# Unread matmuls before the expert work, a new order and half tiles in the last expert, and three more DMA transposes

## The chip, the cores and the metric

The kernel runs on one core of one Trainium2 chip. The core has a matmul engine (TensorE; PE in the profile, with its weight loads as PEld), three engines for elementwise work (VectorE, DVE; ScalarE, ACT; GpSimd, POOL), a sync engine (SP) that mostly issues transfers, and 16 DMA engines. A stretch of queue of an engine is named by a q behind it (SPq). The metric is the time of one execution on the device in microseconds (us), the median of several runs.

## The reference

The first half is an attention with global and local tokens: 8 batches, 8 heads of 64, 32 global and 512 local tokens. A global query sees all keys; a local one sees the global keys and the local keys within 32 places. The second half is a mixture of 8 experts over all 4352 tokens, weighted by a Sinkhorn-normalised router:

```python
k_all = np.concatenate([k_g, k_l], axis=2)
out_g = np.matmul(sm(scale * q_g @ k_all^T), v_all)
mask = np.abs(pos[:, None] - pos[None, :]) <= 32
s_l = np.concatenate([scale * q_l @ k_g^T, np.where(mask, scale * q_l @ k_l^T, -1e9)], axis=-1)
out_l = np.matmul(sm(s_l), v_all)
...
P = np.exp(logits - logits.max())
for _ in range(8):
    P /= P.sum(1, keepdims=True) + 1e-09
    P /= P.sum(0, keepdims=True) + 1e-09
    P *= N / E
for e in range(E):
    out += P[:, e:e + 1] * (np.maximum(x @ w1[e], 0.0) @ w2[e])
```

(The matrix products are shortened here.) Each expert goes from 512 to 1024 to 512 features.

## The kernel before

**Layout.** The tokens stand in 34 tiles of 128: tiles 0 to 31 are the local tokens, four to a batch, and tiles 32 and 33 are the global tokens of all batches. `groups` (L75) makes nine groups of them: eight of four tiles, and group 8 of the two global tiles. `xT` holds the attention's result, turned; `out_nat` holds the sums of the experts in float32, 34 tiles of 128 by 512.

**The attention loop** (L446 to L565) works on 32 pairs of heads, in 35 turns with an order of its own that is written out by hand (`manual_schedule`): each engine runs its instructions in the order in which the loop issues them. In turn i the pair i is loaded and turned (`stage_aq`, `stage_ak`: L288 on TensorE, L293 on VectorE, L305 on ScalarE, and L309 on GpSimd for the zero-padded queries), pair i - 1 gets its scores (`stage_b`, L325 and L326 on TensorE, L329 on VectorE) and exponentials (`stage_e`, L339 on ScalarE), pair i - 2 has its exponentials turned, and pair i - 3 is multiplied with the values (`stage_c`, L365 on TensorE, L369 and L372 on VectorE) and turned back (`stage_d`, L380 and L381). Every second turn does the global queries: scores in even turns (`global_scores`, L387 and L395; `global_exp`, L402; `global_norm`, L409), the rest in odd ones (`global_turn`, L415; `global_out`, L430). In turn 1 VectorE also clears some buffers (L534 to L539).

**Turning the exponentials.** A pair has two heads, hi = 0 and 1. For pairs below `NPE` = 6 both heads are turned by TensorE (`stage_t`, L350, seven transposes), and copied out of PSUM by ScalarE (first head) or VectorE (second head), both in L352. From pair 6 on, `stage_e` issues a DMA transpose from SP (L343) as soon as the head's last exponential stands.

**The expert work in the attention loop.** `fill(1)` stands at eight places of each turn. It takes a piece (two matmuls of 512 columns) of the expert work in `queue`, if there is any. Expert 0's work on a batch enters the queue at the end of the turn that finishes the batch (L518), first in turn 6; so up to there the eight `fill(1)` do nothing. Its PSUM tiles come from the pool `ps_m`, two buffers under the tag `mo`.

**The experts.** Behind the loop come the router's normalisation, with expert work between its steps, and then experts 1 to 7 (L621 to L629). For each expert and each group, `layer1` (L94) makes eight tiles of hidden features, whose ReLU is done by ScalarE (L101) and VectorE (L103) in turns, and `layer2` (L114) makes, for each tile of tokens, eight matmuls of 512 columns into `py`. VectorE adds `py` times the router's weight to `out_nat` (L124). In the last expert `store_tile` then stores the tile from SP: a local tile by one transfer of 256 KB (L81), whose rows are ordered "(p s) d -> s p d" with s = 4 outermost, a global one by four of 64 KB (L85). An expert's weights (L71, L72) are loaded while the one before it computes.

The order of the experts' groups is 0 to 8 for every expert, so the two global tiles are last.

Of the kernel before, what the change touches and what calls it, by code (L numbers as in the profile page):

```python
# [11 lines left out]
FP32 = mybir.dt.float32  # L12
AF = mybir.ActivationFunctionType
ALU = mybir.AluOpType
# [3 lines left out]
P = 128  # L18
# [4 lines left out]
def kernel(  # L23
# [13 lines left out]
    nc = tc.nc  # L37

    B, H, Sl, Dh = q_l.shape
    Sg = q_g.shape[2]  # L40
    D, E = moe_w_gate.shape
# [4 lines left out]
    NJ = Sl // P  # L46
    DP = D // P
    TO = NTOK // P
    FT = F // P
# [11 lines left out]
    out_nat = persist.tile([P, TO, D], FP32)  # L61
    P_nat = persist.tile([P, TO, E], FP32)
    w_gate_sb = persist.tile([P, DP, E], FP16)
    identity = persist.tile([P, P], FP16)
# [9 lines left out]

    groups = [(4 * b, 4) for b in range(B)] + [(4 * B, TO - 4 * B)]  # L75

    def store_tile(t):
        if t < 4 * B:
            b, j = divmod(t, NJ)
            r0 = S * b + Sg + P * j  # L80
            nc.sync.dma_start(out=out[r0 : r0 + P, :].rearrange("(p s) d -> s p d", s=NJ), in_=out_nat[:, t, :])  # L81
        else:
            for i in range(4):
                b = 4 * (t - 4 * B) + i
                nc.sync.dma_start(out=out[S * b : S * b + Sg, :],  # L85
                                  in_=out_nat[Sg * i : Sg * (i + 1), t, :])
# [21 lines left out]
    def layer2(e, w2e, g, ps, tag, hT, copy):  # L108
        t0, gn = groups[g]
        for c in range(gn):  # L110
            t = t0 + c
            py = ps.tile([P, D], FP32, tag=tag, name=f"py{e}_{t}")
            for fk in range(FT):
                nc.tensor.matmul(py, hT[fk][:, P * c : P * (c + 1)], w2e[:, fk, :],  # L114
                                 start=(fk == 0), stop=(fk == FT - 1))
                if fk % 2 == 1 and fk < FT - 1:
                    yield
            if e == 0:
                if copy == "act":
                    nc.scalar.copy(out=out_nat[:, t, :], in_=py)  # L120
                else:
                    nc.vector.tensor_copy(out=out_nat[:, t, :], in_=py)  # L122
            else:
                nc.vector.scalar_tensor_tensor(out=out_nat[:, t, :], in0=py, scalar=P_nat[:, t, e : e + 1],  # L124
                                               in1=out_nat[:, t, :], op0=ALU.mult, op1=ALU.add)
                if e == E - 1:
                    store_tile(t)
            yield
# [3 lines left out]
        yield from layer1(e, wts[e][0], g, ps1, tag1, hp, hT, relu)  # L132
        yield from layer2(e, wts[e][1], g, ps2, tag2, hT, copy)

    queue = []

    def fill(n):
        while n > 0 and queue:
            if next(queue[0], "done") == "done":
                queue.pop(0)  # L140
            else:
                n -= 1

    make_identity(nc, identity)
    wts = [None] * E

    with ExitStack() as actx:
# [7 lines left out]
        ps_m = pool(name="ps_m", bufs=2, space=PSUM)  # L155
        actx.enter_context(tc.manual_schedule())

        NU, NK, NQ, VW, NPE = 4, 3, 2, Dh + 2, 6
        U7 = 7 * P
        OFF, WID = (0, 224, 480, 704), (192, 224, 224, 192)  # L160
        AV = ((("a", 0, 0), ("o", 0, 1)), (("o", 3, 1), ("a", 1, 2), ("o", 1, 3)),
# [99 lines left out]
        for (d0, n, c0, w) in ((0, NJ, WIN, P), (224, NJ - 1, 0, WIN), (128, NJ - 1, WIN + P, WIN)):  # L261
            nc.vector.tensor_copy(out=mgap[:, 0:n, d0 : d0 + w],
                                  in_=mcan[:, c0 : c0 + w].unsqueeze(1).broadcast_to([P, n, w]))
# [70 lines left out]
        def stage_e(p, hi, jp):  # L334
            st, nm = sts.pop((p, hi, jp))
            u = u_buf[(2 * p + hi) % NU]
            for jj in range(2):
                j = 2 * jp + jj
                nc.scalar.activation(out=u[:, OFF[j] : OFF[j] + WID[j]], in_=st[:, jj, 0 : WID[j]], func=AF.Exp,  # L339
                                     scale=-1.0, bias=nm[:, jj : jj + 1])  # L340
            if jp == 1 and p >= NPE:
                uT = awk.tile([P, 7, P], FP16, tag="uT", bufs=5, name=f"uT{p}_{hi}")
                nc.sync.dma_start_transpose(out=uT, in_=u)  # L343
                uTs[2 * p + hi] = uT
# [101 lines left out]
        for i in range(NP + 3):  # L446
# [2 lines left out]
            kt = (i - 3) // 2 if i >= 3 and i % 2 == 1 and (i - 3) // 2 < 2 * B else None  # L449
            ks = (i - 2) // 2 if i >= 2 and i % 2 == 0 and (i - 2) // 2 < 2 * B else None  # L450
            bv, x = divmod(i + 2, 4)
            V = 0 < bv < B

            if Bs:
# [2 lines left out]
            if Bs:  # L457
                stage_b(pb, 0, 1)
                stage_e(pb, 0, 0)
            if 0 <= i - 2 < NPE:  # L460
                stage_t(i - 2, 0)
            fill(1)
            if C:
                stage_c(pc)
            if Bs:
                stage_b(pb, 1, 0)
                stage_e(pb, 0, 1)
            if 0 <= i - 2 < NPE:
                stage_t(i - 2, 1)
            if i == 0:  # L470
                load_pair("k", k_l, 2)
# [3 lines left out]
            if A:  # L475
                stage_aq(pa)
                if i > 0:
                    order("q", i + 1)
            if V and x in (1, 2):
                load_va(bv, x + 1)  # L480
# [14 lines left out]
            if ks is not None:  # L495
                if ks == 0:
                    qg_transposes(qs)
                gsu[ks] = global_scores(ks)
            if V and x < 2:
                load_va(bv, x)  # L500
            if V and x == 3:
                load_vo_edges(bv)
# [40 lines left out]
            if i in (1, 2):  # L543
                c = slice(512 * (i - 1), 512 * i)
                nc.gpsimd.dma_start(out=wts[0][0][:, :, c], in_=moe_w1[0][:, c].rearrange("(dko dki) f -> dki dko f", dki=P))
            elif i in (4, 5):
                c = 4 * (i - 4)
                nc.gpsimd.dma_start(out=wts[0][1][:, c : c + 4, :],
                                    in_=moe_w2[0][P * c : P * (c + 4)].rearrange("(fko fki) d -> fki fko d", fki=P))
            if 8 <= i < 14:  # L550
                d, src = ((skg, k_g), (svg, v_g), (sqg, q_g))[(i - 8) // 2]
# [17 lines left out]
    with tc.tile_pool(name="wpool2", bufs=1) as wpool2, \  # L569
         tc.tile_pool(name="hx", bufs=34) as hx, \  # L570
         tc.tile_pool(name="ps_h", bufs=3, space=PSUM) as ps_h, \
         tc.tile_pool(name="ps_y", bufs=4, space=PSUM) as ps_y, \
         tc.tile_pool(name="ps_k", bufs=1, space=PSUM) as ps_k, \
         tc.manual_schedule():

        wts[1] = load_weights(1, wpool2)
        for g in range(B - 1, len(groups)):
            queue.append(both(0, g, ps_h, "ph", ps_y, "py", hx, "act", "act"))
        NPRE = 3
        pre = [[] for _ in range(NPRE)]  # L580
        for g in range(NPRE):
            queue.append(layer1(1, wts[1][0], g, ps_h, "ph", hx, pre[g], "act"))

        gm = sink.tile([P, 1], FP32, tag="gm")
        nc.vector.reduce_max(out=gm, in_=P_nat, axis=AX.XY)
        gmb = sink.tile([P, P], FP32, tag="gmb", bufs=1)
        nc.vector.tensor_scalar(out=gmb, in0=ones_mat, scalar1=gm, scalar2=None, op0=ALU.mult)
        fill(4)
        pgm = ps_k.tile([P, P], FP32, tag="pk", name="pgm")
        nc.tensor.matmul(pgm, gmb, ident32, start=True, stop=True)  # L590
        gma = sink.tile([P, 1], FP32, tag="gma")
        nc.vector.reduce_max(out=gma, in_=pgm, axis=AX.X)
        gmn = sink.tile([P, 1], FP32, tag="gmn")
        nc.vector.tensor_scalar(out=gmn, in0=gma, scalar1=-1.0, scalar2=None, op0=ALU.mult)
        fill(2)
        nc.scalar.activation(out=P_nat, in_=P_nat, func=AF.Exp, bias=gmn)

        ratio = float(NTOK) / float(E)
        for it in range(8):
            rs = sink.tile([P, TO, 1], FP32, tag="rs")  # L600
            nc.vector.reduce_sum(out=rs, in_=P_nat, axis=AX.X)  # L601
            nc.vector.tensor_scalar(out=rs, in0=rs, scalar1=1e-9, scalar2=None, op0=ALU.add)
            nc.vector.reciprocal(out=rs, in_=rs)  # L603
            nc.vector.tensor_tensor(out=P_nat, in0=P_nat, in1=rs.broadcast_to([P, TO, E]), op=ALU.mult)  # L604
            cp = sink.tile([P, E], FP32, tag="cp")
            nc.vector.reduce_sum(out=cp, in_=P_nat.rearrange("p t e -> p e t"), axis=AX.X)  # L606
            fill(8)
            pcs = ps_k.tile([P, E], FP32, tag="pk", name=f"pcs{it}")
            nc.tensor.matmul(pcs, ones_mat, cp, start=True, stop=True)  # L609
            fill(1)  # L610
            cr = sink.tile([P, 1, E], FP32, tag="cr")
            nc.vector.tensor_scalar(out=cr[:, 0, :], in0=pcs, scalar1=1e-9, scalar2=1.0 / ratio,
                                    op0=ALU.add, op1=ALU.mult)
            nc.vector.reciprocal(out=cr, in_=cr)
            nc.vector.tensor_tensor(out=P_nat, in0=P_nat, in1=cr.broadcast_to([P, TO, E]), op=ALU.mult)  # L615
        for t in range(TO):
            eng = nc.vector if t < 2 else nc.gpsimd
            eng.tensor_scalar(out=out_nat[:, t, :], in0=out_nat[:, t, :], scalar1=P_nat[:, t, 0:1],  # L618
                              scalar2=None, op0=ALU.mult)
        fill(1 << 30)  # L620
        for e in range(1, E):  # L621
            if e > 1:
                wts[e] = load_weights(e, wpool2 if e % 2 else wpool)
            for g in range(len(groups)):
                if e == 1 and g < NPRE:
                    queue.append(layer2(1, wts[1][1], g, ps_y, "py", pre[g], "dve"))
                else:
                    queue.append(both(e, g, ps_h, "ph", ps_y, "py", hx, "both"))
                fill(1 << 30)  # L629
# [30 lines left out]
```

## Time and profile before

| | |
|---|---|
| median of 3 runs | 1091.76 us (1091.75 to 1091.79) |
| the profiled execution | 1095.55 us, of which its span is 1093.7 |
| mean granted TensorE clock in it | 0.993 |
| TensorE busy | 1054.3 us (96%), 6734 matmuls |
| VectorE, ScalarE, GpSimd busy | 559.7, 331.1 and 239.6 us (51%, 30%, 22%) |
| all matmuls of `layer1` (L94) and of `layer2` (L114) | 499.1 and 495.9 us |
| DMA traffic | 56.27 MB, mean 51 GB/s |

The span runs from the first to the last instruction of the profiled execution. In the profile's tables a window row has its bounds and length, then for each engine its busy time and the number of instructions, then the granted clock (PEclk, 1.00 is full), the mean share of the 16 DMA engines that was busy (where it exceeds 1, transfers overlap on an engine), and GB/s. A timeline row has its start, its time, engine, line, operation, output and input, a count, and in brackets the idle time before it with what ended that. A row of waits has who waited for whom, the sum, the count and the longest.

### The profile page before, as it was taken

The page shows a single profiled execution, that of the slowest core. Times are in us where ns is not written, and L with a number is a line of the kernel's source. Part 1 is how long each engine was busy: PE and PEld are TensorE (multiplying, and loading weights), DVE is VectorE, ACT ScalarE, POOL GpSimd, SP SyncE. Part 2 cuts the span into 40 slices and gives each one's busy share as a digit, 9 for nine tenths or more (in the row PEclk, how much of TensorE's full clock was granted, in tenths as well). Part 3 has the DMA queues.
Part 4 walks back from the last instruction along what each step waited for, and adds up shares of the span by engine and source line. Part 5 has one row for each costly group of instructions (what it writes and reads, how often), then busy time and mean ns, then how long its engine had stood idle before and what let it go on. Part 6 is the DMA issues. An engine that isn't in the chain of part 4 may idle for free.

```text
span 1093.7 us, 17193 instructions
## 1 busy us (share of the span) xinstructions
PE 1054.3 (96%) x6734; PEld 540.0 (49%) x6734; DVE 559.7 (51%) x1361; ACT 331.1 (30%) x683; POOL 239.6 (22%) x300
## 2 busy tenths in 40 slices
PE   4799999999999999999999999999999999999997
PEld 3666666655444544445444544454444444454443
DVE  6888888867244444444444444444444444444443
ACT  6767777754311111112111111111111111111111
POOL 8977788610990000000000000000000000000000
PEclk9899999999999999999999999999999999999999
DMA  9999999951003030004000400022000400002222
GB/s 159 136 137 159 139 140 141 126 88 25 1 11 68 12 66 1 1 1 78 0 1 1 78 1 1 1 35 44 1 1 1 77 1 1 1 10 77 76 77 90
DMA packets 126210, 56.27 MB, mean 51 GB/s; under 512 B 90800, under 2 KB 117680, under 8 KB 126128
## 3 DMA queue, kind: packets, MB, share of 16 engines
q0 software_dynamic: 64304, 28.98, 22.4%
q1 hardware_dynamic: 60736, 25.53, 11.9%
q8 instruction: 53, 0.87, 0.3%
q10 hardware_dynamic: 1088, 0.66, 0.3%
q14 instruction: 29, 0.24, 0.1%
HBM read 60.31 MB, written 8.91 MB: 63 GB/s over the span
## 4 chain that ended last, share of the span: by engine, by line
PE 78%; DVE 1%; issue 0%; ACT 0%; ACTq 0%; DVEq 0%
PE py L114 39%; PE ph L94 39%; DVE st L329 0%; PE po L365 0%; PE pcs L609 0%; DVE cp L606 0%; DVE out_nat L122 0%; PE pog L430 0%; DVE P_nat L604 0%; DVE P_nat L615 0%; DVE rs L601 0%; PE px L380 0%; DVE rs L603 0%; DVE out_nat L124 0%; DVE gm L395 0%
## 5 line engine op out<-in xcount | busy, mean ns | idle before, releaser
L94 PE MATMUL ph<-xT,w1e 128*128 128x512 f16 (+1 forms) x2304 | 499.1, 368 | 0.4 <-DVE P_nat L442 0.4
L114 PE MATMUL py<-w2e,ht 128*128 128x512 f16 x2176 | 495.9, 379 | 0.0
L101 ACT ACTIVATE ht<-ph 128x512 f16<-128x512 f32 (+1 forms) x336 | 192.7, 573 | 686.5 <-PE ph L94 686.0
L94 PEld LDWEIGHTS <-w1e 128*128 128x128 f16 x2304 | 219.5, 98 | 220.6 <-issue 0.4
L114 PEld LDWEIGHTS <-ht 128*128 128x128 f16 x2176 | 207.3, 98 | 231.9
L124 DVE SCALAR_TENSOR_TENSOR out_nat<-py,P_nat,out_nat 128x512 f32<-128x512 f32 x238 | 178.6, 750 | 248.2 <-PE py L114 247.2
L103 DVE TENSOR_SCALAR ht<-ph 128x512 f16<-128x512 f32 (+1 forms) x240 | 158.5, 660 | 226.4 <-PE ph L94 224.6
L71 POOL DMA_DIRECT2D w1e<-in_moe_w_dram x7 | 5.4, 770 | 510.0 <-PE ph L94 505.4
L339 ACT ACTIVATE u<-st,nm 128x192 f16<-128x192 f32 (+1 forms) x256 | 104.0, 461 | 37.3 <-DVE nm L329 26.0
L329 DVE CUSTOM_DVE_ANT_0 st<-s,mask 128x192 f32<-128x192 f32 (+1 forms) x256 | 82.3, 368 | 4.7 <-PE s L326 3.1
L618 POOL TENSOR_SCALAR out_nat<-out_nat,P_nat 128x512 f32<-128x512 f32 x32 | 49.6, 1575 | 36.5 <-DVE P_nat L615 36.5
L325 PE MATMUL s<-kT,qTz 128*128 128x160 f16 (+1 forms) x256 | 44.7, 245 | 6.7 <-DVE nm L329 2.9
L309 POOL COPY qTz<-qT 64x512 f16<-64x512 f16 x60 | 36.7, 612 | 38.1 <-ACT qT L305 36.0
L326 PE MATMUL s<-kgT,qTz 128*128 128x32 f16 x256 | 37.1, 183 | 0.0
L325 PEld LDWEIGHTS <-qTz 128*128 128x128 f16 x256 | 25.9, 101 | 14.9 <-DVE nm L329 3.2
L326 PEld LDWEIGHTS <-qTz 128*128 128x128 f16 x256 | 25.0, 98 | 10.3 <-issue 2.2
L365 PEld LDWEIGHTS <-uT 128*128 128x128 f16 x640 | 24.4, 99 | 9.4 <-issue 3.1
L409 POOL TENSOR_SCALAR ug<-ug,gr 128x544 f16<-128x544 f16 x16 | 26.5, 1658 | 10.2 <-DVE gr L408 9.7
L197 POOL DMA_DIRECT2D va<-in_v_l_dram x32 | 28.7, 901 | 0.0
L365 PE MATMUL po<-va,uT 128*128 128x65 f16 x256 | 25.5, 196 | 2.0 <-ACT ug L402 1.9
L372 DVE TENSOR_TENSOR xn<-po,rc 128x512 f16<-128x512 f32 x32 | 22.1, 691 | 1.1
L293 DVE COPY kT<-pk 128x512 f16<-128x512 f16 x32 | 22.0, 686 | 0.2 <-PE pk L288 0.2
(107 smaller groups left out, 472.8 us busy)
## 6 DMA issues: line engine op xcount, KB each, us to landing
out_dram<-out_nat SPq DMA_DIRECT2D x32, 256.0 KB
w1e<-in_moe_w_dram POOLq DMA_DIRECT2D x7, 1024.0 KB, 7.9
w2e<-in_moe_w_dram POOLq DMA_DIRECT2D x7, 1024.0 KB, 10.1
va<-in_v_l_dram POOLq DMA_DIRECT2D x32, 128.0 KB, 4.7
kr<-in_k_l_dram POOLq DMA_DIRECT2D x30, 128.0 KB, 4.4
qr<-in_q_l_dram POOLq DMA_DIRECT2D x30, 128.0 KB, 4.5
w1e<-in_moe_w_dram POOLq DMA_DIRECT2D x2, 512.0 KB, 7.1
w2e<-in_moe_w_dram POOLq DMA_DIRECT2D x2, 512.0 KB, 7.3
```

What stands on the lines that cost most here:

```text
L94: nc.tensor.matmul(ph[:, 0:N], w1e[:, dk, P * fm : P * (fm + 1)], xT[:, dk, P * t0 : P * t0 + N], start=(dk == 0), stop=(dk == DP - 1))
L101: nc.scalar.activation(out=ht[:, 0:N], in_=ph[:, 0:N], func=AF.Relu)
L103: nc.vector.tensor_scalar(out=ht[:, 0:N], in0=ph[:, 0:N], scalar1=0.0, scalar2=None, op0=ALU.max)
L114: nc.tensor.matmul(py, hT[fk][:, P * c : P * (c + 1)], w2e[:, fk, :], start=(fk == 0), stop=(fk == FT - 1))
L124: nc.vector.scalar_tensor_tensor(out=out_nat[:, t, :], in0=py, scalar=P_nat[:, t, e : e + 1], in1=out_nat[:, t, :], op0=ALU.mult, op1=ALU.add)
L309: nc.gpsimd.tensor_copy(out=qTz_buf[2 * (p % NQ) + hi][r], in_=qT[r])
L325: nc.tensor.matmul(ps[:, jj, w0 : w0 + k1 - k0], lhsT, kT[:, k0:k1], start=True, stop=True)
L326: nc.tensor.matmul(ps[:, jj, g0 : g0 + Sg], lhsT, kg, start=True, stop=True)
L329: nc.vector.tensor_tensor_reduce(out=st[:, jj, 0 : WID[j]], in0=ps[:, jj, 0 : WID[j]], in1=mask[:, OFF[j] : OFF[j] + WID[j]], scale=-scale ...
L339: nc.scalar.activation(out=u[:, OFF[j] : OFF[j] + WID[j]], in_=st[:, jj, 0 : WID[j]], func=AF.Exp, scale=-1.0, bias=nm[:, jj : jj + 1])
L365: nc.tensor.matmul(po[:, hi, W * j : W * (j + 1)], uT[:, blk, :], v[:, x, 2 * hp + hi, 0:W], start=(n == 0), stop=(n == len(AV[j]) - 1))
L618: eng.tensor_scalar(out=out_nat[:, t, :], in0=out_nat[:, t, :], scalar1=P_nat[:, t, 0:1], scalar2=None, op0=ALU.mult)
```

## The change

There are three edits.

1. *Unread matmuls.* From turn 1 to turn 6, a `fill(1)` that finds no expert work issues four 128-column matmuls of the identity with itself into a tile of the pool `ps_m`. Nothing reads the result. That is 8 units a turn and 48 in all, 192 matmuls. In turn 7 the list is emptied.
2. *The last expert.* In expert 7 group 8, with the global rows, comes first, and groups 0 to 7 follow. The last tile is then tile 31; it is computed in two halves of 256 columns, each with its own eight matmuls, its own addition on VectorE and its own store of 128 KB.
3. *DMA transposes.* `NPE` becomes (6, 3): first heads are turned by TensorE up to the sixth pair as before, second heads only up to the third. So the second heads of pairs 3, 4 and 5 (counted from 0) go by DMA transpose from SP.

```diff
-    def store_tile(t):
+    def store_tile(t, c0=0, c1=D):
...
-            nc.sync.dma_start(out=out[r0 : r0 + P, :].rearrange("(p s) d -> s p d", s=NJ), in_=out_nat[:, t, :])
+            nc.sync.dma_start(out=out[r0 : r0 + P, c0:c1].rearrange("(p s) d -> s p d", s=NJ),
+                              in_=out_nat[:, t, c0:c1])
...
+            if e == E - 1 and t == 4 * B - 1:
+                for c0 in range(0, D, D // 2):
+                    h = slice(c0, c0 + D // 2)
+                    for fk in range(FT):
+                        nc.tensor.matmul(py[:, h], hT[fk][:, P * c : P * (c + 1)], w2e[:, fk, h],
+                                         start=(fk == 0), stop=(fk == FT - 1))
+                    nc.vector.scalar_tensor_tensor(out=out_nat[:, t, h], in0=py[:, h], scalar=P_nat[:, t, e : e + 1],
+                                                   in1=out_nat[:, t, h], op0=ALU.mult, op1=ALU.add)
+                    store_tile(t, c0, c0 + D // 2)
+                yield
+                continue
...
-    queue = []
+    queue, warming = [], []
...
+        while n > 0 and warming:
+            pw = warming[0].tile([P, 512], FP32, tag="mo", name=f"pw{len(warming)}")
+            warming.append(pw)
+            for c in range(4):
+                nc.tensor.matmul(pw[:, P * c : P * (c + 1)], identity, identity, start=True, stop=True)
+            n -= 1
...
-        NU, NK, NQ, VW, NPE = 4, 3, 2, Dh + 2, 6
+        NU, NK, NQ, VW, NPE = 4, 3, 2, Dh + 2, (6, 3)
...
-            if jp == 1 and p >= NPE:
+            if jp == 1 and p >= NPE[hi]:
...
+            if i == 1:
+                warming.append(ps_m)
+            elif i == 7:
+                warming.clear()
...
-            if 0 <= i - 2 < NPE:
+            if 0 <= i - 2 < NPE[0]:
                 stage_t(i - 2, 0)
...
-            if 0 <= i - 2 < NPE:
+            if 0 <= i - 2 < NPE[1]:
                 stage_t(i - 2, 1)
...
-            for g in range(len(groups)):
+            order_g = list(range(len(groups)))
+            for g in order_g if e < E - 1 else order_g[-1:] + order_g[:-1]:
```

## The prediction

> **What bounds the kernel now.** I read the page's slices first, then the windows cut at the turns of the attention loop, then TensorE's timeline, and for the end the SP queue's timeline, its waits and windows over the output stores.
>
> ```profile
> PEclk9899999999999999999999999999999999999999
> ```
>
> TensorE is busy 96% of the span, so two places are open: the first 60 us, where the granted clock falls, and what follows the last matmul. Turn i of the loop begins with its first score matmul (L325); the windows are turns 1 to 9 in order.
>
> ```profile
> core 0: us, PE busy (x) PEld busy (x) DVE busy (x) ACT busy (x) POOL busy (x), PEclk, DMA share, GB/s
> 9.71:13.77 4.06, 2.58 (x25) 2.16 (x25) 3.64 (x18) 3.66 (x8) 4.06 (x6) 1.00 1.36 143
> 13.77:22.90 9.13, 5.38 (x47) 4.18 (x46) 6.55 (x24) 6.65 (x17) 9.07 (x15) 1.00 1.62 158
> 22.90:30.47 7.57, 5.62 (x90) 5.15 (x89) 6.25 (x25) 5.66 (x14) 7.36 (x11) 0.77 1.18 135
> 30.47:35.62 5.15, 3.92 (x74) 3.33 (x69) 4.88 (x23) 4.07 (x10) 5.09 (x8) 1.00 1.38 159
> 35.62:42.77 7.15, 4.60 (x88) 3.94 (x88) 6.35 (x26) 5.29 (x13) 7.00 (x10) 1.00 1.00 105
> 42.77:49.44 6.67, 4.50 (x89) 3.81 (x85) 5.94 (x25) 4.96 (x12) 6.15 (x11) 0.93 1.21 184
> 49.44:59.54 10.10, 9.97 (x109) 7.16 (x106) 5.96 (x26) 6.24 (x15) 6.65 (x9) 0.71 0.80 94
> 59.54:65.56 6.02, 6.02 (x70) 3.88 (x69) 5.33 (x23) 5.33 (x13) 4.94 (x8) 1.00 1.39 153
> 65.56:72.98 7.42, 6.64 (x91) 4.48 (x90) 5.65 (x26) 5.28 (x14) 7.25 (x11) 1.00 1.22 149
> ```
>
> Turns 3 to 6 are VectorE's and GpSimd's (DVE 6.25 of 7.57, POOL 7.36 of 7.57); TensorE stands idle for 13.1 us of turns 1 to 6. From turn 7 on expert matmuls fill it, and turn 7 takes 10.10 us where turn 9, with the same kinds of steps, takes 7.42: its clock is 0.71, because the stretch before it was thin:
>
> ```profile
> 45.07:48.49 3.42, 1.88 (x23) 1.35 (x22) 3.42 (x12) 3.07 (x8) 3.02 (x5) 1.00 1.27 198
> ...
> 8.34 0.59 PE L288 MATMUL pk<-identity,k 128*128 128x128 f16 x4
> ...
> 34.44 0.38 PE L288 MATMUL pk<-identity,k 128*128 128x128 f16 x4 [0.62 <-ACT qT L305]
> ```
>
> The two rows of four 128-column matmuls are the same work at the half and the full clock (before 20 us the page has no clock record and prints 1.00; the durations say half). The end:
>
> ```profile
> 1067.30:1069.90 2.60, 2.60 (x13) 1.18 (x12) 0.92 (x2) 1.04 (x2) 0.00 (x0) 1.00 0.26 87
> 1069.90:1072.50 2.60, 2.60 (x14) 1.18 (x13) 1.16 (x2) 0.77 (x2) 0.00 (x0) 1.00 0.26 101
> 1072.50:1075.10 2.60, 2.60 (x14) 1.19 (x13) 0.94 (x2) 0.42 (x1) 0.00 (x0) 1.00 0.25 98
> 1075.10:1076.90 1.80, 1.80 (x10) 0.86 (x9) 0.82 (x2) 0.00 (x0) 0.00 (x0) 1.00 0.08 31
> ...
> 1074.86 0.75 DVE L124 SCALAR_TENSOR_TENSOR out_nat<-py,P_nat,out_nat 128x512 f32<-128x512 f32 x1 [1.03 <-PE py L114]
> ...
> 1075.63 0.54 SPq L81 DMA_DIRECT2D out_dram<-out_nat  x1
> ...
> 1080.81 0.54 SPq L81 DMA_DIRECT2D out_dram<-out_nat  x1
> ...
> 1086.98 0.75 DVE L124 SCALAR_TENSOR_TENSOR out_nat<-py,P_nat,out_nat 128x512 f32<-128x512 f32 x1 [0.98 <-PE py L114]
> ...
> 1090.47 0.32 SPq L85 DMA_DIRECT2D out_dram<-out_nat  x1
> ...
> SPq L85 <- DMA out_dram<-out_nat: 1.3, 1, 1.3
> ```
>
> The windows stand in a layer-1 stretch without new stores, after a group's four 256 KB stores, the last issued at 1067.00. They drain at some 100 GB/s with a DMA share of 0.25: four of 16 engines, 2.6 us a tile, while TensorE makes a tile in 1.73 us (L124 at 1061.04, 1062.77, 1064.49, 1066.22). So the fourth store is behind the other three. The last three lines price that: the store of tile 31, issued at 1080.81, is what the last L85 store waits for (same semaphore), until 1090.47, 9.66 us after its issue. That backlog now lies under the last group's 7 us of matmuls.
>
> **The change part by part.** The sum goes against the profiled execution (span 1093.7, 1.85 us around it, 1095.55 in all); the median is 3.79 below it, and I carry differences over unchanged.
>
> *Order and halves in the last expert.* TensorE: 16 matmuls of 256 columns for 8 of 512; L94's 256-column rows are 0.109 us apart (3.49 us for 32), 16 make 1.74 against 1.73: nothing. The global group after its own predecessor in expert 6 needs its activations (0.38 ACT, 0.42 DVE) in turns every 0.87 us: covered, and its eight 64 KB stores move ahead of the 32 tile stores on SP, which sits idle there: nothing. Expert 7's weights are asked for about 117 us earlier: nothing; without that cover a load shows 7.9 and 10.1 us. The cost is behind the last matmul. Tile 28's L124 now begins three tiles before the last, at 1086.98 - 3 x 1.73 = 1081.79, its store 0.77 later (1074.86 to 1075.63) at 1082.56. A whole tile 31 would land as long after it as now: 1090.47 - 1075.63 = 14.84, so at 1097.40. The halves are issued near 1086.8 and 1087.4, while the four engines work on tiles 29 and 30, so the earlier start buys nothing. No half store is in this trace. Bounds: half the time of a whole one each (2.6 together, landing 1097.4) to as long as a whole one each (5.2, landing 1100.0). The DMA packet records have 84 ns for the stores' 2 KB packets and 46 to 54 ns for 1 KB packets of the first loads; 32 packets an engine at 46 to 54 give 1.5 to 1.7 a half, 2.9 to 3.5 the pair: landing 1097.7 to 1098.3; I take 1098.0. What SP, GpSimd and the barrier do behind the last landing takes 1.6 us now (landing record 1092.1, end 1093.7), 1.35 with the last store's semaphore last in SP's row of waits: end 1099.4. **Term: +5.7 us** (bounds +5.0 and +7.9).
>
> The Trainium skill (DMA: Bandwidth & Descriptors, "Why a DMA increments its semaphore by 16 and not by 1") says that a hardware-queue copy uses the largest number of engines up to 16 that divides both sides' slowest dimension, and the lowest-numbered ones: four for [4, 32, 256] as for [4, 32, 512]. The share of 0.25 agrees for whole tiles; by that rule the halves join the same backlog.
>
> *Unread matmuls.* 8 units a turn in turns 1 to 6, 48 in all, of four 128-column matmuls into the pool `mo`. From the two L288 rows, less one matmul's latency of 0.19 to 0.29, a unit holds TensorE for 0.25 us at full and 0.42 at half clock. All serial it would be 12 to 20 us, against 13.1 idle: bounds 0 and +7 before any gain. Step by step: in turn 1, at half clock, four units stand ahead of the last scores and keys (L326, L288), which come 1.1 us later; VectorE loses 0.8 of it, and its 3 us of memsets (L534, L535) move with it. In turn 2 one unit before the scores and one before the global query turn add some 0.4 and 0.3. ACT's qgP copies (L280) wait for that turn, and the global maximum for them: turn 3 starts +1.4. In turns 4 and 6 three or four units ahead of `po` (L365) bring it 0.4 to 0.5 late for VectorE's L369 (due 44.63, done 44.32 now, 0.7 later then). In turns 3 and 5 TensorE waits 0.8 to 1.1 for ACT at that spot, which hides them. Sum: +2.3. For it, the 45.07 window gets about 13 units more, so turn 7 starts warm. Turn 3's half-clock loss is 7.57 - 7.15 = 0.4, but VectorE sets that turn: nothing taken.
>
> *Second heads by DMA, pairs 4 to 6.* Three times 7 transposes (0.43) leave TensorE and a copy of 0.62 (L352 DVE) leaves VectorE, in turns 5, 6, 7. VectorE sets turns 5 and 6, where about 0.5 a copy counts once POOL (7.00 of 7.15) and the late `po` are allowed for 0.8 in both. Three DMA transposes (1.23 us each on SP, landing after 3.3 to 6.8) are needed over a turn after ACT wrote `u`: covered; uncovered, up to 6 us for one. One stands ahead of the edge loads (L210, L211), due two turns on.
>
> *Turn 7.* It starts at 49.44 + 2.3 - 0.8 = 50.9. At full clock I take turn 9's 7.42, plus the remaining L350 group of 0.44, less half of turn 9's 0.78 idle: 7.5; end 58.4 against 59.54. From there TensorE is the bound, and the shift goes through. **Term: -1.1 us** (bounds -5.0, below, and +4.5: the +7 with turn 7's 2.6 back).
>
> **Sum:** +5.7 - 1.1 = +4.6; 1091.76 + 4.6 = 1096.4 us.
>
> By the Trainium skill (TensorE: Matmul & The Clock Gate, "The HAM clock gate") it takes an idle window of some 3.4 us to halve the clock. The trace differs: the clock fell at 48.5 after a 3.42 us window with 1.88 busy. By that rule as by the trace the filled windows stay warm.
>
> **The rivals.** *A, not slower:* the units cost nothing and all gains count: turn 7 at 7.1 (-3.0), turn 3 (-0.4), two VectorE copies (-1.1), a warm turn 2 (-0.5): -5.0, total +0.7, 1092.5. For it: 13.1 us idle; against it: the units sit between steps that VectorE waits for. It decides from an early gain of 3.5 us on. *B, half stores as long as whole ones:* +2.0 on the forecast, 1098.4; for it speaks that a packet's time may not scale with size when writing to DRAM; against it the 46 to 54 ns. *C, the fillers bind:* each turn 2 to 6 is 0.5 us longer than I have it, +2.5: 1098.9; the waits of each unit on TensorE's own semaphore for its bank speak for it. *D, the clock falls anyway:* turn 7 keeps 9.7 us, +2.2: 1098.6; against it, the window 38.25 to 41.66 held the clock at 1.94 busy of 3.41.
>
> **How the numbers follow.** Forecast 0.62, A 0.09, B 0.12, C 0.12, D 0.05. A change under 0.2% (2.2 us) can't be told from none here. Forecast, B, C and D are slower: 0.91, less 0.02 for a forecast with more early gain; A gives same, with 0.03 beyond it on the fast side. So faster 0.03, same 0.08, slower 0.89. The range goes from between A and the forecast, 1093.2, to past C, 1099.6.
>
> **What would show it.** Right: L81's last store issued with three before it undrained, windows at 100 GB/s and a share of 0.25 for some 10 us after the last matmul, which ends about 1 us earlier than now; PEclk 9 in the 49 to 59 window; turn 3 late. Wrong: a share above 0.3 behind the last L124 (A's side), turn 7 beginning before 49.4, or PEclk still under 0.9 in turn 7.

## The result, and the profile after

The changed kernel takes 1100.04 us at the median of six executions, before 1091.76. One of the six, the profiled one, ran with TensorE's clock granted at 0.95 and took 1135.76 us; the median of the other five is 1099.72, 8.0 us slower than before (a ratio of 1.0072 with a 95% interval of 1.0059 to 1.0086), and the lines here are of e1, a second profile of the same kernel (1098.16 us, span 1096.4). In a second set (e1 below) it was 1099.46 against 1092.30, 1.0065 (1.0051 to 1.0079). Slower was forecast, but by 4.6 us, with an upper end at 1099.6; so the time lies outside the range.

The clock line of e1's page:

```profile
PEclk9999999999999999999999999999999999999998
```

The dip of before's first profile (an 8 in the second slice) is not there, though within turns 1 and 2 the mean clock is only 0.89. Windows of the changed kernel (e1), cut at turn 1, turn 3, turn 7, turn 8, turn 32 (the last one with scores), the start of VectorE's last addition, and the end:

```profile
core 0: us, PE busy (x) PEld busy (x) DVE busy (x) ACT busy (x) POOL busy (x), PEclk, DMA share, GB/s
9.20:25.09 15.89, 12.05 (x134) 11.23 (x134) 11.26 (x43) 10.46 (x25) 15.08 (x24) 0.89 1.44 154
25.09:50.70 25.61, 22.65 (x441) 20.97 (x438) 21.98 (x96) 19.42 (x46) 23.27 (x32) 1.00 1.11 128
50.70:57.66 6.96, 6.85 (x102) 4.80 (x99) 5.31 (x25) 5.94 (x15) 6.62 (x9) 1.00 1.48 163
57.66:221.86 164.20, 154.99 (x1989) 103.27 (x1988) 140.81 (x587) 121.41 (x292) 125.53 (x173) 1.00 1.15 143
221.86:1086.30 864.44, 861.26 (x4248) 406.63 (x4246) 373.87 (x587) 169.75 (x302) 62.74 (x47) 1.00 0.14 28
1086.30:1096.38 10.08, 0.00 (x0) 0.00 (x0) 0.48 (x1) 0.00 (x0) 0.00 (x0) 0.69 0.22 81
```

The same stretches in a second profile of the kernel before (e5, 1091.58 us, span 1089.8):

```profile
9.46:22.87 13.41, 8.41 (x71) 6.39 (x71) 10.06 (x42) 9.95 (x25) 13.29 (x20) 1.00 1.53 147
22.87:49.36 26.49, 18.88 (x326) 16.36 (x324) 23.39 (x98) 19.64 (x47) 25.11 (x36) 1.00 1.16 143
49.36:56.73 7.37, 7.24 (x109) 5.27 (x106) 5.78 (x26) 6.10 (x15) 6.70 (x9) 1.00 1.05 135
56.73:220.46 163.73, 154.80 (x1989) 103.19 (x1988) 140.72 (x587) 121.53 (x292) 125.18 (x172) 1.00 1.19 140
220.46:1084.15 863.69, 861.08 (x4240) 405.86 (x4238) 373.39 (x585) 169.76 (x302) 62.75 (x47) 1.00 0.14 28
1084.15:1089.80 5.65, 0.00 (x0) 0.00 (x0) 0.75 (x1) 0.00 (x0) 0.00 (x0) 0.88 0.42 124
```

The column to read is the length behind each pair of bounds:

| stretch | before, first profile | before, second (e5) | after (e1) | after, as predicted | e1 less e5 |
|---|---|---|---|---|---|
| turns 1 and 2 | 13.19 | 13.41 | 15.89 | 14.6 | +2.5 |
| turns 3 to 6 | 26.54 | 26.49 | 25.61 | 26.6 | -0.9 |
| turn 7 | 10.10 | 7.37 | 6.96 | 7.5 | -0.4 |
| turns 8 to 31 | 163.76 | 163.73 | 164.20 | 163.8 | +0.5 |
| turn 32 to the end | 870.39 | 869.34 | 874.52 | 876.1 | +5.2 |

The loss has two parts, the end (+5.2) and turns 1 and 2 (+2.5; turns 3 to 7 are 1.3 shorter). The +0.5 in turns 8 to 31 stands in every profile with edit 3 (164.2 us or more, without it 163.7 to 163.8), most of it in turns 11 and 21 (0.26 and 0.19); why was not followed. And the second profile of before shows no slow turn 7. The end of the changed kernel, in windows (e1):

```profile
1083.80:1086.40 2.60, 1.88 (x16) 1.28 (x14) 1.34 (x3) 0.00 (x0) 0.00 (x0) 1.00 0.24 83
1086.40:1089.00 2.60, 0.00 (x0) 0.00 (x0) 0.38 (x1) 0.00 (x0) 0.00 (x0) 1.00 0.26 102
1089.00:1091.60 2.60, 0.00 (x0) 0.00 (x0) 0.00 (x0) 0.00 (x0) 0.00 (x0) 0.73 0.27 103
1091.60:1094.20 2.60, 0.00 (x0) 0.00 (x0) 0.00 (x0) 0.00 (x0) 0.00 (x0) 0.50 0.26 94
1094.20:1096.30 2.10, 0.00 (x0) 0.00 (x0) 0.00 (x0) 0.00 (x0) 0.00 (x0) 0.50 0.03 11
```

and its timeline there:

```profile
1081.14 6.21 SPq L81 DMA_DIRECT2D out_dram<-out_nat  x5
...
1084.68 0.48 DVE L120 SCALAR_TENSOR_TENSOR out_nat<-py,P_nat,out_nat 128x256 f32<-128x256 f32 x1
1085.22 1.03 PE L118 MATMUL py<-w2e,ht 128*128 128x256 f16 x8 [0.58 <-DVE out_nat L120]
1086.30 0.48 DVE L120 SCALAR_TENSOR_TENSOR out_nat<-py,P_nat,out_nat 128x256 f32<-128x256 f32 x1 [1.13 <-PE py L118]
```

No engine computes after 1086.8, and some 100 GB/s go out at a share of 0.26 up to 1094.2: the backlog that the prediction described. The bracket in the PE row is new: the second half's matmuls waited 0.58 us for VectorE to read the first half, which stands in the same PSUM tile.

### The profile page after: what moved, and what is told of

The parts are those of the page before. It is cut to its first block, busy times and chain, and to the rows that moved or that the text cites. A ratio compares the mean times of both kernels' runs of the same rounds, so it can differ in the third digit from the quotient of the medians.

```text
span 1134.0 us, 17555 instructions
## 1 busy us (share of the span) xinstructions
PE 1097.2 (97%) x6913; PEld 557.8 (49%) x6913; DVE 560.1 (49%) x1359; ACT 330.8 (29%) x683; POOL 239.4 (21%) x300
## 4 chain that ended last, share of the span: by engine, by line
PE 79%; DVE 1%; issue 0%; ACT 0%; ACTq 0%; DVEq 0%
PE py L126 39%; PE ph L95 39%; DVE st L347 0%; PE py L118 0%; PE po L383 0%; PE pcs L631 0%; DVE cp L628 0%; DVE out_nat L134 0%; PE pog L448 0%; DVE out_nat L120 0%; DVE P_nat L626 0%; DVE P_nat L637 0%; DVE rs L623 0%; PE px L398 0%; DVE rs L625 0%
## 5 line engine op out<-in xcount | busy, mean ns | idle before, releaser
L95 PE MATMUL ph<-xT,w1e 128*128 128x512 f16 (+1 forms) x2304 | 516.9, 378 | 0.4 <-DVE P_nat L460 0.4
L126 PE MATMUL py<-w2e,ht 128*128 128x512 f16 x2168 | 513.4, 390 | 0.0
L95 PEld LDWEIGHTS <-w1e 128*128 128x128 f16 x2304 | 223.8, 100 | 233.3 <-issue 0.5
L126 PEld LDWEIGHTS <-ht 128*128 128x128 f16 x2168 | 210.9, 100 | 244.2
L343 PEld LDWEIGHTS <-qTz 128*128 128x128 f16 x256 | 25.5, 100 | 14.6 <-DVE nm L347 3.5
```

Of the source, the lines that this page charges most:

```text
L95: nc.tensor.matmul(ph[:, 0:N], w1e[:, dk, P * fm : P * (fm + 1)], xT[:, dk, P * t0 : P * t0 + N], start=(dk == 0), stop=(dk == DP - 1))
L343: nc.tensor.matmul(ps[:, jj, w0 : w0 + k1 - k0], lhsT, kT[:, k0:k1], start=True, stop=True)
```

## The experiments

Two theories of the miss stood at the start: that the start of the kernel loses what it should have gained ("start"), or that the end costs 8 us instead of 5.7 ("end"). Each diff is against the kernel before unless it says otherwise, and shows its main lines only. Each set has its own runs of before beside it (medians 1091.6 to 1093.0), and a difference is against these. The profiles' turns, from first score matmul to first score matmul, stand in a table under e7.

**e1: the changed kernel once more.** No edit.

> The changed kernel unchanged, for a profile at the full clock. Both theories: some 8 us slower than before (1100). The record before the result had +5.7 us for the end and -1.1 for the start. Theory 'start' says the end is near its +5.5 and turn 7 begins late enough that its end comes about 3 us later than before (near 62.5 instead of 59.5). Theory 'end' says turn 7 ends at 58 to 59.5 and the time from the last expert's tile 28 to the end of the span is 8 us longer than before.

1099.46 us, before 1092.30. Turn 7 ends at 57.66 and the stretch from turn 32 on is 5.2 us longer. So "end" falls; but turn 7's end does not fit "start" either in the number I gave, which was made from the first profile of before.

**e2: edit 2 alone** (order and halves in the last expert).

```diff
+            order_g = list(range(len(groups)))
+            for g in order_g if e < E - 1 else order_g[-1:] + order_g[:-1]:
...
+            if e == E - 1 and t == 4 * B - 1:
...
```

> The kernel before with edit 2 alone (global group first in the last expert, last tile in halves). Theory 'start': 5.2 to 5.8 us slower than before, about 1097.4. Theory 'end': about 8 us slower, 1099.8, all of the change's loss.

1097.09 us, 1.0046 (1.0032 to 1.0060): +4.8 us, as "start" had it.

**e3: edits 1 and 3 alone** (the change without the lines of e2).

> The kernel before with edits 1 and 3 (unread matmuls in turns 1 to 6, second heads by DMA from the fourth pair on). Theory 'start' (the fillers bind): 2.5 to 3 us slower, about 1094.5. Theory 'end': -1.1 to 0.2 us against before, 1090.7 to 1092.

1093.76 us, 1.0012 (1.0004 to 1.0021): +1.5 us. It is slower, where my term was -1.1, by less than "start" had; turns 1 and 2 take 16.25 us, turns 3 to 6 take 25.60, turn 7 takes 6.96.

**e4: edit 1 alone.**

```diff
+            if i == 1:
+                warming.append(ps_m)
+            elif i == 7:
+                warming.clear()
```

> The kernel before with edit 1 alone. By my steps the DMA transposes are worth 0.8 us in turns 5 and 6 and 0.4 in turn 7, so this is about 1 us slower than edits 1 and 3 together under both theories: 1095.5 under 'start', 1092 under 'end'. If the three transposes on SP cost time instead, this one is faster than both together.

1094.39 us, 1.0021 (1.0012 to 1.0030): +2.1. Turns 1 and 2 take 17.08 us, turns 3 to 6 take 26.44 (before, e5, 26.49), turn 7 takes 7.37. So the loss of edit 1 lies in turns 1 and 2. That turns 3 to 6 come out even is a balance and not the absence of a cost: behind the longer turn 2, turn 3 is 0.7 shorter than in e5, turn 4 is 0.47 longer and turn 6 0.19. Edit 3 is worth 1.08 in turns 5 and 6 (e3 against this one) and 0.41 in turn 7.

**e5: the kernel before once more.** The profile of e2, whose attention loop is that of before, had a turn 7 of 7.38 us at full clock, and a half-clock window at 41.6 instead. That gave a new theory: where such windows fall is chance, and the first profile of before, at 1095.55 against a median of 1091.76, was an unlucky execution ("phase").

> The kernel before unchanged, for a second profile. In the profile of edit 2 alone, whose attention loop is that of before, the clock fell at 41.6 for one window and turn 7 took 7.38 us at full clock, where the first profile of before had 10.10 at half clock. Theory 'phase' (where the half-clock windows fall is chance, the first profile of before was an unlucky one at 1095.55 against a median of 1092): turn 7 takes 7.3 to 7.6 us here and the execution 1091 to 1092.5. Theory 'always' (before loses turn 7's clock in every execution and the fillers win it back): turn 7 takes about 10 us here too.

1091.58 us, turn 7 in 7.37 us, full clock from 26.9 us to 1088.4. "Phase" holds. The three other profiles of the same loop (e2, e8 and e9) have turn 7 at 7.37 as well; in e2 and e8 one half-clock window fell in turn 6 and cost some 0.9. The runs of before bear it out: of the 27 beside e9 to e11, 21 have a mean granted clock of 0.998 or more and take 1091.1 to 1092.9 us; six have 0.994 or 0.995 and take 1094.0 to 1094.4. In the two earlier sets it is 2 of 20 and 4 of 21 with 0.996 or less. That these executions lost turn 7 is inferred from their times; none of them was profiled. So the clock that the unread matmuls were to win back there is lost in a tenth to a fifth of the executions, and a loss of that size does not enter the median.

**e6: edit 3 alone.**

```diff
-        NU, NK, NQ, VW, NPE = 4, 3, 2, Dh + 2, 6
+        NU, NK, NQ, VW, NPE = 4, 3, 2, Dh + 2, (6, 3)
```

> The kernel before with edit 3 alone. From the profiles: turns 3 to 6 with edits 1 and 3 took 25.60 us, with edit 1 alone 26.44, and turn 7 took 6.96 against 7.37. Theory 'phase': edit 3 is worth 0.8 + 0.4 = 1.2 us and nothing is lost without the fillers: 1091 to 1091.3, 1.2 us faster than before. Theory 'always': turn 7 stays at half clock, so 1092 to 1093, not faster than before by over 0.5.

1092.88 us, 0.9996 (0.9987 to 1.0006): no change. That is the number of "always" but not its mechanism, for in the profile (1091.26 us) turn 7 takes 6.97 us at full clock. Against e5's profile, turns 5 and 6 gain 1.07 and turn 7 gains 0.40, as "phase" had it, but turns 8 to 31 lose 1.05, of which 0.57 stands in turn 10. Besides, the clock falls more often: seven of the eleven runs have a mean clock of 0.996 or less, against 4 of the 21 of before beside them, and six of the seven take 1092.9 to 1094.6 (the other 1091.23). That the missing transposes are the cause of that is not shown: TensorE's busy share in turn 5 is no lower without them (4.37 of 6.69 us, e5 4.60 of 7.15).

**e7: edits 1 and 3 with the unread matmuls from turn 3 on** (against the changed kernel, without edit 2).

```diff
-            if i == 1:
+            if i == 3:
                 warming.append(ps_m)
```

> Edits 1 and 3, with the unread matmuls from turn 3 on instead of turn 1. Theory 'turns 1 and 2' (the loss of the fillers lies there: turns 1 and 2 took 15.9 to 17.1 us in the three profiles with them, 13.2 and 13.4 without; turns 3 to 6 lost nothing): turns 1 and 2 back at 13.4, about 1.2 us faster than before, 1091, and 2.5 us faster than with all fillers. Rival 'every turn': only a third of the loss goes, 1092.5 to 1093.

1091.98 us, 0.9992 (0.9981 to 1.0003): 1.1 us under before, within what can be told from none, and 2.6 us better against before than e3 (-1.1 and +1.5). Turns 1 and 2 take 13.41 again, so the main loss of edit 1 lies there. All eleven runs have a mean clock of 0.998 or more, where e6, the same kernel without the fillers, has four such; so from turn 3 on the fillers hold the clock. They do not do it for nothing: turns 3 to 6 take 26.42 us, in e6 25.42. The turns of five profiles in us:

| turn | before (e5) | edit 3 (e6) | edit 1 (e4) | edits 1 and 3 (e3) | fillers from turn 3, edit 3 (e7) |
|---|---|---|---|---|---|
| 1 | 4.06 | 4.06 | 5.16 | 5.03 | 4.06 |
| 2 | 9.35 | 9.36 | 11.92 | 11.21 | 9.35 |
| 3 | 7.55 | 7.56 | 6.85 | 7.09 | 7.91 |
| 4 | 5.15 | 5.15 | 5.62 | 5.62 | 5.62 |
| 5 | 7.15 | 6.69 | 7.14 | 6.59 | 6.59 |
| 6 | 6.64 | 6.03 | 6.83 | 6.30 | 6.30 |
| 7 | 7.37 | 6.97 | 7.37 | 6.97 | 6.97 |

Turn 4 shows the mechanism: VectorE's reciprocal of `po` follows its neighbours at once in e5, and waits for TensorE behind the units in e3:

```profile
32.28 0.20 DVE L369 RECIPROCAL rc<-po 128x8 f32<-128x8 f32 x1
...
34.77 0.21 DVE L387 RECIPROCAL rc<-po 128x8 f32<-128x8 f32 x1 [0.27 <-PE po L383]
```

From turn 1 to the start of turn 32 e7 takes 210.98 us, e5 211.00: at full clock it gains nothing there.

**e8: edit 2 without the halves** (against e2).

```diff
-            if e == E - 1 and t == 4 * B - 1:
+            if False:
```

> Edit 2 without the halves: global group first in the last expert, tile 31 whole. With the halves the last expert's matmuls ended 0.85 us later (the second half's first matmul waited 0.58 us for VectorE's reading of the first half), and the two half stores landed 1.36 us apart, 2.7 together against 2.6 for a whole store. Theory 'backlog' (the four DMA engines set the end): the store side gains 0.1 only, the wait of TensorE does not matter since the stores are behind by several us: 1096.9 to 1097.1, 4.7 us slower than before. Rival 'halves cost': 0.85 us better than edit 2 in full, 1096.2.

1097.97 us, 1.0048 (1.0035 to 1.0061): +4.9 us, as with the halves (+4.8). From turn 32 to the end it takes 874.55 us, e2 874.71. The halves neither help nor harm while the stores are behind: "backlog".

**e9: the last group's stores by 32 rows** (against e8).

```diff
+            if t >= 4 * (B - 1):
+                dst = out[r0 : r0 + P, c0:c1].rearrange("(p s) d -> s p d", s=NJ)
+                for s in range(NJ):
+                    nc.sync.dma_start(out=dst[s], in_=out_nat[32 * s : 32 * (s + 1), t, c0:c1])
+                return
```

> The kernel of e8 (global group first in the last expert, tile 31 whole, no other edit) with one more change: the four tiles of the last group are stored by four transfers of 32 rows each instead of one with the dimension of 4 outermost. A 32-row store of before (L85) landed 1.6 us after its issue when nothing stood ahead of it. Theory 'backlog' (the whole loss of edit 2 is the queue on four DMA engines): tile 31's last transfer is issued some 2.4 us after the last L136 begins and lands 1.6 later, the span ends 5.4 to 5.6 us after that L136 as in before's second profile (5.65), so 1092.5 to 1093.2, within 0.2% of before and 5 us under e8. Rival 'order' (the reordering itself costs, through the seam between experts 6 and 7 or the stores' bandwidth): 1096 to 1098.

1091.87 us, 0.9995 (0.9986 to 1.0004), like before, where e8 lost 4.9 us. Its windows from the last group's first store on:

```profile
1079.23:1081.80 2.57, 2.57 (x14) 1.17 (x12) 0.75 (x1) 0.00 (x0) 0.00 (x0) 1.00 0.41 104
1081.80:1084.40 2.60, 1.79 (x9) 0.59 (x7) 1.50 (x2) 0.00 (x0) 0.00 (x0) 1.00 0.53 137
1084.40:1087.00 2.60, 0.00 (x0) 0.00 (x0) 0.00 (x0) 0.00 (x0) 0.00 (x0) 1.00 0.54 141
1087.00:1089.20 2.20, 0.00 (x0) 0.00 (x0) 0.00 (x0) 0.00 (x0) 0.00 (x0) 0.87 0.12 30
```

The share goes to 0.54, over the 0.25 of four engines, and the span ends 5.6 us after the last addition began (1083.63 to 1089.24). So the order itself costs nothing that can be told, and the whole loss of e8 is the queue on four engines. The Trainium skill (DMA: Bandwidth & Descriptors, "Why a DMA increments its semaphore by 16 and not by 1") lets the slowest dimension choose the number of engines; with 32 in place of 4 the trace agrees, its share being 0.54.

**e10: what is left to gain** (the changed kernel with e7's `i == 3`, whole tiles, and e9's stores, the first two from SP and the last two from ACT).

> Unread matmuls from turn 3 on, edit 3, global group first, tile 31 whole, and the last group's stores by 32-row transfers, two from SP and two from ACT. e7 measured 1.1 us under before for the first two; the four transfers cost two issues instead of four on each queue, 0.8 us less than e9. So 1.5 to 2.2 us faster than before, 1090.8 to 1091.5. If the order still cost something, 1093 or more.

1090.84 us, 0.9989 (0.9979 to 0.9998): 1.5 us under before, and under both kernels. By the profile, 0.7 of it is at the end, with the issues on two queues (the span ends 4.90 us after the last addition began, in e9 5.61); up to turn 32 nothing is gained (211.12 us from turn 1, e5 211.00).

**e11: a cast out of turn 1** (against e3).

```diff
-                nc.vector.tensor_copy(out=ident32, in_=identity)
...
+            if i == 20:
+                nc.vector.tensor_copy(out=ident32, in_=identity)
```

> Edits 1 and 3 as in e3, with VectorE's cast of the identity (128x128 to float32) taken out of turn 1's end and put in turn 20. In the profiles with fillers in turn 1 this cast took 0.70 to 0.85 us, in those without 0.16, and a GpSimd copy ran at that moment. Theory 'collision' (VectorE waits for GpSimd's copy): turn 2's score step on VectorE comes 0.7 to 0.85 us earlier than in e3, and the kernel is 0.7 us faster than e3, about 0.8 us slower than before. Rival: another instruction at that spot waits instead and nothing moves.

The rows that led to it, VectorE's timeline of e3 (the cast, the first score step of turn 2, its last one, and the global maximum):

```profile
17.55 0.85 DVE L561 CAST ident<-identity 128x128 f32<-128x128 f16 x1
18.32 0.34 DVE L347 CUSTOM_DVE_ANT_0 st<-s,mask 128x192 f32<-128x192 f32 x1
...
22.02 0.39 DVE L347 CUSTOM_DVE_ANT_0 st<-s,mask 128x224 f32<-128x224 f32 x1 [1.26 <-PE s L344]
...
25.16 0.72 DVE L413 TENSOR_REDUCE gm<-sa 128x1 f32<-128x544 f32 x1 [1.86 <-PE sa L409]
```

GpSimd's of e3 at that moment:

```profile
17.04 0.72 POOL L204 COPY q<-qr 128x512 f16<-128x512 f16 x1
17.59 0.71 POOL L204 COPY k<-kr 128x512 f16<-128x512 f16 x1
```

and VectorE's of e11, the clearing of `ones_mat`, the same first score step, the same maximum:

```profile
17.41 0.17 DVE L560 MEMSET ones_mat<- 128x128 f32 x1
17.49 0.29 DVE L347 CUSTOM_DVE_ANT_0 st<-s,mask 128x192 f32<-128x192 f32 x1
...
24.17 0.72 DVE L413 TENSOR_REDUCE gm<-sa 128x1 f32<-128x544 f32 x1 [2.16 <-PE sa L409]
```

The score step comes 0.83 us earlier and the maximum 0.99; turn 1 begins 0.19 earlier (9.20, 9.39) and turn 2 0.06 (14.36, 14.42). So at that point of turn 2 some 0.7 us of the delay was this cast. Little of it is left at the start of turn 3 (25.21, in e3 25.64): here the clock was half from 20.11 to 26.93 us, in e3 only from 19.47 to 22.88. The median is 1092.77, +0.4 against before (1.0003, 0.9994 to 1.0012), where e3, in another set, had +1.5.

**e12: the change in full, with e9's stores.**

> The changed kernel in full, halves included, with the stores of the last group as 32-row transfers as in e9. Theory 'two parts' (the loss is the store queue, some 5 us, plus turns 1 and 2, some 1.5 to 2): the first is gone and the second stays, 1093.3 to 1094.2 where before has 1092.3, 5.5 to 6 us under the changed kernel. Rival 'together': the parts cost more together than apart (7.2 to 8.3 measured against 4.8 + 1.5), and 1094.5 to 1095.5 remains.

1095.04 us, 1.0030 (1.0018 to 1.0042): +3.4. The rival's interval has it, though not for the rival's reason. Its turn 32 starts at 222.09, 1.6 us after e5's; from there to the end it takes 871.15 us, e9 869.28. So once the stores are no longer behind, the halves do cost, 1.9 us. The issues of the last group's stores on SP, here and then in e9:

```profile
1081.37 9.24 SPq L84 DMA_DIRECT2D out_dram<-out_nat  x20
...
1079.23 7.38 SPq L84 DMA_DIRECT2D out_dram<-out_nat  x16
```

In both they begin 0.8 us after the group's first addition began (1080.60 and 1078.45), follow each other at 0.46 us, and the span ends 2.63 us after the last of them is issued (1090.61 and 1086.61). The last tile has eight issues instead of four, and those four are the 1.86 us between the two rows. TensorE's wait of 0.58 is not on this path: the second half's addition is over at 1087.01, its first issue is at 1088.86.

## Why the prediction was wrong, step by step

*The sum's basis.* This is the step that failed: "I carry differences over unchanged", and with it the gain in turn 7 within the term of -1.1. The profiled execution was 3.79 us over the median, and 2.7 of that was the very turn 7 (10.10 against 7.37) from which I drew the gain; another 1.1 lay behind the last addition (6.71 against 5.65). Against the typical execution the term for the start is not -1.1 but -1.1 + 2.7 = +1.6, and e3 measured +1.5. That the two agree so well is luck: the fillers cost 3.0 us up to the end of turn 7 (e3 against e6) where the sum has 2.3, and edit 3 gains 1.5 in turns 5 to 7 (e6 against e5) where, taken from e5, it has 0.7. Taken against the profiled execution's own time the forecast was 1095.55 + 4.6 = 1100.15, and the changed kernel has 1099.72 and 1099.46; that too is closer than the single terms were.

*Turn 7 at full clock, 7.5 us:* right as a length (6.96 and 7.37 with and without edit 3), and wrong as a gain. The reason given for its half clock, a thin stretch before it, holds for the execution in which it was read; what it missed is that the same stretch keeps the clock in most others (see the last section).

*A unit's time:* 0.38 and 0.59 less 0.19 and 0.29 give 0.19 and 0.30, not the 0.25 and 0.42 that the prediction uses. In e3 a unit holds TensorE for 0.22 us at full clock (32.94 to 33.16) and 0.38 to 0.43 at half (9.74 to 10.12, 20.89 to 21.32), so the figures used were near, though not by that working.

*Turns 1 and 2, +1.4:* too small, +2.5 (e1) to +3.7 (e4, 17.08 less 13.41), of which turn 3 gives back 0.5 to 0.7. The chain was as written: the units ahead of the scores, the memsets, the query copies, the global maximum. Two things were missing: the cast that grew from 0.16 us to 0.85 in e3 (0.46 in e12), and the clock, which fell again in turn 2 after TensorE had waited for VectorE (3.2 us up to 19.04 in e3, then half clock from 19.5 to 22.9; in e4 from 20.6 to 27.5), so that its units cost 0.42 each.

*Turns 4 and 6, `po` late by 0.9 in all:* right in mechanism, 0.7 in size (0.47 in turn 4, 0.19 to 0.27 in turn 6). The cost does not show in the sum of turns 3 to 6 (26.44 against 26.49, e4) because turn 3 is shorter there. Where turn 2 is not late (e7), turn 3 loses 0.35, which the prediction took as hidden.

*Edit 3, -0.8 in turns 5 and 6:* too small, 1.07 (e6 against e5), and 0.40 in turn 7. The sum has nothing for the 0.45 that turns 11 and 21 lose in the profiles with it. Alone it gains nothing at the median (e6).

*The end, +5.7:* the mechanism right (e8, e9), the size +5.2 by profile and +4.8 by medians. The pair of half stores took 2.7 us (landing records 1.36 apart), where I took 3.3; and in the first profile a group's four stores took 14.84 us from the first issue to the last landing, in e5 13.77.

*TensorE, "nothing":* 0.8 us, from the wait between the halves (from turn 32 to the last matmul's end 864.4 us in e1 and e2, without halves 863.6 in e8). It was hidden by the backlog.

*The rivals.* C (the fillers bind) named the right edit; it spread the loss over turns 2 to 6, where most of it lies in turns 1 and 2. A (all gains count) fell on the same mistake as the forecast: its largest item was turn 7. B and D were wrong: the pair of half stores took 2.7 us and not 5.2, and turn 7 took 6.96.

*What stays open.* The parts measured apart give 4.8 + 1.5 = 6.3 us, the whole 7.2 and 8.0. e1's profile accounts for 6.6 against e5's. Executions of the changed kernel with a mean clock of 0.992 to 0.995 are frequent (6 of 10), and where they lose the clock was not profiled. Nor is it known why edit 3 costs time in turns 11 and 21, or why e6 loses the clock so often.

## What to carry to other kernels

Set the profiled execution's time beside the median before using any of its rows as a gain: if it is 0.3% longer, find out which rows make it so, for those gains are not in the median. Before the last tile is chosen, look at how long its store lands after its issue, not at how early it is issued; a small outermost dimension of the transfer confines it to few DMA engines, and the stores queue. Splitting the last tile's store adds issues, and these follow each other on their queue. Fillers that keep the clock up cost little where TensorE waits for others anyway (up to 0.5 us a turn here), and much where TensorE's next step is what the others wait for (2.5 to 3.7 us in turns 1 and 2).

## What was not expected of the hardware

A VectorE cast of 128x128 took 0.16 us in seven of the eight profiles without fillers in turn 1 (0.38 in e7) and 0.46 to 0.92 in the five with them in which it stands there (0.79, 0.85 and 0.70 in e1, e3 and e4); in e3 it ran beside GpSimd's copies of 0.7 us. The other profiles fit: wherever it took 0.16 us it was over at least 0.27 before the first of these copies began (in e5 at 16.81, the copy at 17.08), and in the five slow ones it began during the first copy and ended 0.1 after the end of one of the two (in e3 at 18.40, the second copy at 18.30). Only e7's, which began 0.25 before the first copy, fits neither. The profile names no releaser, so that it waits for them is argued, not shown; moving it away removed the time (e11). The Trainium skill (SBUF — State Buffer, "SBUF: two separate sides") says that VectorE in its two-port modes and GpSimd share one port pair as an exclusive lock; the numbers agree with that, though no run here shows in which mode this cast ran.

The clock fell after windows in which TensorE was far from idle (1.88 busy of 3.42 us in before's first profile) and stayed up in the same code in other executions (e5). What decides it can be read from the traces. The granted clock changes at the edges of windows of 3.41 us, in all fourteen profiles. Up to the last matmul it fell after eleven of these windows, in which TensorE was busy for 0.30 to 1.88 us (1.73 in e2 and 1.72 in e8, the ones that cost turn 6), and after none of the more than 4000 others at full clock, of which the thinnest had 1.94 (before, 38.25 to 41.66). Where the windows fall on the code differs between executions: the one that cost turn 7 in before began 2.30 us into turn 6 (45.07), in e5 one began 1.25 us into it (43.97) and had 2.27. Between turns 3 and 7 e5's thinnest window had 2.08, and with the fillers e7's had 2.48. So this stretch is close to the edge, as the prediction saw, and one profile cannot tell how often an execution falls on which side of it.
